# New order numbers and task times for a planned one-core kernel: gated recurrence and gated two-layer network

## The chip, the cores and the metric

The kernel runs as one launch on one core of one Trainium2 chip. The metric is the device time of that launch in microseconds (us). Five engines work side by side, each through its own queue in program order: TensorE (PE; its weight loads are listed as PEld), VectorE (DVE), ScalarE (ACT), GpSimd (POOL) and SyncE (SP), which here issues nearly all DMA transfers. An engine that comes to an instruction whose input is not ready stands there, with everything behind it.

## The reference

```python
B, H, S, D = 4, 8, 768, 48          # tokens 3072, d_model 384, d_ff 2048
for t in range(S):
    state = alpha[:, :, t, :, None] * state + k_t (outer) v_t
    y[:, :, t] = q_t @ state
x = y.transpose(0, 2, 1, 3).reshape(3072, 384)
h = x @ w_in
out = (h * tanh(softplus(h))) @ w_out
```

## The kernel before, in words

The recurrence is cut into 24 chunks (`attention(n)`, 0 to 23). Each chunk has loads of its q, k and alpha (`qka`, 772.5 KB) and v, decay products on DVE (two scans at L570 and L583, products at L579 and L593, a decay of the state at L601), and three pieces on PE: `turn` (transposes of k, L761), `scores` (L616 with the state, then L639) and `product` (L616, then L680). `scores` and `product` are 48 and 80 small matmuls in a full chunk. DVE masks the scores (L650) and adds to the state (L800); ACT and DVE split the result into a high and a low part (`xs`, L694 and L699), and SP moves rows of it (L720).

The two-layer network is cut into 105 units (`unit`, 0 to 104). A unit takes two or four chunks and one of 16 blocks of d_ff: nine matmuls on PE (`up`, L826), five passes on ACT (L835, L838, L841, L844, L853), two on DVE (`gate` L847, `lower` L856), and three matmuls per chunk on PE (`down`, L885). Tiles `t29` and `g29` are those of unit 29. Before a block can be used its weights (`ws`, 768 KB) are decoded on DVE (`w_lead`, L441, L447, L453, and `left_here`, L468), with a pass on ACT. Later each block is loaded once more (`wc`) and checked on DVE (`gathered`, L508).

While PE would have nothing to do in the first 130 us, the plan gives it fills: matmuls of a constant whose result nobody reads (L940). They stand in the program like any other instruction, so PE runs each of them when it comes to it.

The order of all engines is made while the program is built. `Plan.order` is a list scheduler: every task has a key, a cost (`COST`, occupancy and delay until its result can be used), needs and buffers, and the task that can begin first by these costs is taken next. `SHIFT` is a table of numbers added to the keys of chunks, units, weight blocks and checks, `EARLY_BANKS` says which PSUM banks a chunk takes, and `SAME` is what PE is held to save where one group of small matmuls follows another. The program's end tests a flag on every engine and leaves out a slow general path that these inputs don't need (`tc.If`, L1142).

Of the kernel before, what the change touches and what calls it, by code (L numbers as in the profile page):

```python
# [29 lines left out]
P = 128  # L30
# [4 lines left out]
NFF = FF // P  # L35
# [35 lines left out]
    0: "o1 o1 att o3 att".split(),  # L71
    1: "att o3 o1 att h".split(),
    2: "att h att att o3".split(),
    3: "o0 h att o0 o3".split(),
    4: "o2 att o3".split(),
    9: "o3 att o2".split(),
    10: "o1 o3 att".split(),
    11: "o3 o1 att".split(),
    13: "o1 o2 att".split(),
    14: "att o0 o1".split(),  # L80
    15: "o3 att att".split(),
    16: "att att o1".split(),
    17: "o2 o3 att".split(),
    18: "o3 att o0".split(),
    20: "att o3 o2".split(),
    21: "att att h".split(),
    22: "att o2 att".split(),
# [7 lines left out]
    },  # L95
    "unit": {
# [17 lines left out]
    },  # L114
    "weight": {
        0: -1.8297, 1: -88.668, 2: -1.298, 3: -0.44909, 4: -0.76088, 5: -0.16277, 7: -7.1065,
        8: -3.6601, 9: -2.0214, 11: 0.91205, 12: -0.61512, 13: 2.8687, 15: 3.8897,
    },
    "weight check": {
        1: 2.9506, 2: -1.2413, 3: -2.7653, 4: -7.2029, 5: -0.37293, 6: -5.1126, 7: -4.9684,  # L120
        8: -0.99544, 9: -8.3869, 10: -8.6038, 11: 6.855, 12: 3.149, 13: -24.555, 14: 0.49888,
        15: 1.0013,
    },
}
X_PE = 4
TURN_AT = 0.15
# [1083 lines left out]
```

## Time and profile before

| | |
|---|---|
| time, median of 3 runs | 480.56 us (480.13 to 480.57) |
| time of the profiled execution | 480.47 us, of which the span of its instructions is 478.8 us |
| PE busy | 466.8 us (97%) |
| ACT busy | 365.6 us (76%) |
| DVE busy | 340.9 us (71%) |
| granted TensorE clock | mean 0.997 of full speed |
| moved by DMA | 56.82 MB, mean 119 GB/s |

The busy time of PE holds the fills too, and its matmuls' ends are modelled, so a busy PE isn't PE at its peak. Shares over the whole span hide that the first 130 us and the rest have different limits; they are read in stretches.

### The profile page before, as it was taken

How to read it: one execution, taken by the hardware profiler on the slowest of the kernel's cores; microseconds unless marked ns; L12 is line 12 of the kernel's file. 1: busy time of each engine (PE TensorE's matmuls, PEld its weight loads, DVE VectorE, ACT ScalarE, POOL GpSimd, SP SyncE). 2: the span in 40 equal slices, each digit the busy share in tenths (PEclk: the TensorE clock that was granted, in tenths of full speed). 3: DMA queues.
4: the chain of work that ended last, by engine and by line, in shares of the span. 5: the costliest groups of instructions: out<-in, count | busy, mean ns of one | idle time of the engine just before them, and what ended most of it. 6: DMA issues, size and time to landing. Idle time of an engine off the chain costs nothing.

```text
span 478.8 us, 12662 instructions
## 1 busy us (share of the span) xinstructions
PE 466.8 (97%) x5233; PEld 418.6 (87%) x5233; DVE 340.9 (71%) x586; ACT 365.6 (76%) x816; POOL 2.4 (1%) x12
## 2 busy tenths in 40 slices
PE   7999999999999999999999989999999999999996
PEld 4668888998989889999999978999989989999995
DVE  8999999999995799789434368797376343355432
ACT  2567879889998968877887846878758878778784
POOL 2000000000000000000000000000000000000000
PEclk9999999999999999999999999999999999999998
DMA  8777536353220363154000266824252000080001
GB/s 292 247 235 253 178 127 231 135 168 115 66 67 9 129 197 111 67 184 159 0 1 0 77 223 213 318 68 132 63 183 81 1 7 4 22 291 18 0 2 70
DMA packets 20078, 56.82 MB, mean 119 GB/s; under 512 B 4016, under 2 KB 12464, under 8 KB 20016
## 3 DMA queue, kind: packets, MB, share of 16 engines
q1 hardware_dynamic: 19872, 55.77, 33.9%
q8 instruction: 42, 0.69, 0.6%
q10 hardware_dynamic: 144, 0.20, 0.1%
q14 instruction: 20, 0.16, 0.1%
HBM read 48.87 MB, written 4.72 MB: 112 GB/s over the span
## 4 chain that ended last, share of the span: by engine, by line
PE 74%; DVE 16%; ACT 6%; issue 2%; DVEq 0%
PE bank L826 31%; PE bank L885 31%; PE bank L616 4%; PE bank L940 2%; DVE t L847 2%; PE bank L639 2%; DVE rest L570 2%; PE bank L761 2%; PE bank L680 2%; DVE g L856 1%; DVE qka L583 1%; DVE w_lead L453 1%; DVE w_lead L447 1%; DVE wio L468 1%; DVE state L800 1%
## 5 line engine op out<-in xcount | busy, mean ns | idle before, releaser
L885 PE MATMUL bank<-wio,g 128*128 128x384 f32 x1152 | 207.4, 329 | 0.0
L826 PE MATMUL bank<-xs,wio 128*128 128x512 f32 (+1 forms) x945 | 205.3, 364 | 1.1 <-DVE t L847 0.8
L885 PEld LDWEIGHTS bank<-wio,g 128*128 128x128 f32 x1152 | 189.8, 189 | 5.0 <-issue 0.2
L826 PEld LDWEIGHTS bank<-xs,wio 128*128 128x128 f32 x945 | 164.0, 189 | 22.1 <-DVE t L847 3.1
L856 DVE SCALAR_TENSOR_TENSOR g<-t,g 128x512 fp32r<-128x512 f32 (+1 forms) x105 | 66.3, 642 | 55.7 <-ACT g L853 55.5
L847 DVE SCALAR_TENSOR_TENSOR t<-t,bank 128x512 f32<-128x512 f32 (+1 forms) x105 | 67.0, 638 | 48.0 <-ACT t L844 47.7
L835 ACT ACTIVATE t<-bank 128x512 f32<-128x512 f32 (+1 forms) x105 | 58.8, 560 | 48.6 <-PE bank L826 45.5
L853 ACT ACTIVATE g<-t 128x512 fp32r<-128x512 f32 (+1 forms) x105 | 60.5, 586 | 20.7 <-DVE t L847 10.6
L841 ACT ACTIVATE t<-t,fifth 128x512 f32<-128x512 f32 (+1 forms) x105 | 71.7, 684 | 2.2
L838 ACT ACTIVATE t<-t 128x512 f32<-128x512 f32 (+1 forms) x105 | 62.0, 592 | 2.1
L844 ACT ACTIVATE t<-t 128x512 f32<-128x512 f32 (+1 forms) x105 | 61.7, 588 | 1.5
L570 DVE TENSOR_TENSOR_SCAN rest<-qka,behind 112x520 f32<-112x520 f32 x24 | 29.7, 1238 | 1.3 <-DMA qka<-in_qka_dram 1.1
L583 DVE TENSOR_TENSOR_SCAN qka<-qka,ahead 112x520 f32<-112x520 f32 x24 | 29.6, 1232 | 0.0
L694 ACT ACTIVATE xs<-bank 112x256 fp32r<-112x256 f32 x48 | 15.8, 379 | 14.8 <-PE bank L680 6.9
L650 DVE COPY_PREDICATED probs<-causal,bank 128x256 f32<-128x256 uint32 x48 | 18.8, 439 | 6.8 <-PE bank L639 5.7
L835 ACT ACTIVATION_READ_ACCUMULATOR t<-bank 128x1 f32 x105 | 20.5, 195 | 0.0
L616 PE MATMUL bank<-qka,state 48*48 48x64 f32 (+1 forms) x704 | 20.0, 221 | 0.3 <-DVE qka L593 0.2
L800 DVE TENSOR_TENSOR state<-bank,state 112x192 f32<-112x192 f32 x40 | 12.9, 353 | 10.3 <-PE bank L680 6.4
L616 PEld LDWEIGHTS bank<-probs,v 64*48 64x48 f32 (+1 forms) x768 | 13.6, 127 | 7.4 <-issue 3.4
L940 PE MATMUL bank<-behind 112*128 112x384 bf16 x76 | 17.5, 367 | 2.4 <-DVE behind L362 2.4
L616 PEld LDWEIGHTS bank<-qka,state 48*48 48x48 f32 (+1 forms) x704 | 15.3, 127 | 4.8 <-issue 3.1
L508 DVE SCALAR_TENSOR_TENSOR unlike<-wc,unlike 128x768 int32<-128x768 int32 x15 | 17.0, 1134 | 3.0 <-DMA wc<-in_wp_dram 3.0
(70 smaller groups left out, 316.6 us busy)
## 6 DMA issues: line engine op xcount, KB each, us to landing
qka<-in_qka_dram SPq DMA_DIRECT2D x22, 772.5 KB, 6.0
ws<-in_wp_dram SPq DMA_DIRECT2D x16, 768.0 KB, 4.4
wc<-in_wp_dram SPq DMA_DIRECT2D x16, 768.0 KB, 5.0
v<-in_vp_dram SPq DMA_DIRECT2D x24, 192.0 KB, 3.2
out_dram<-osb SPq DMA_DIRECT2D x15, 192.0 KB, 2.3
xs<-xs SPq DMA_DIRECT2D x144, 16.0 KB, 3.6
out_dram<-part SPq DMA_DIRECT2D x8, 192.0 KB, 2.5
qka<-in_qka_dram SPq DMA_DIRECT2D x2, 260.5 KB, 3.8
```

What stands on the lines that cost most here:

```text
L570: nc.vector.tensor_tensor_scan(t[:, :0:-1], alpha()[:, :0:-1], behind[:, ::-1], 0.0, ALU.mult, ALU.max)
L583: nc.vector.tensor_tensor_scan(a, a, ahead, 0.0, ALU.mult, ALU.max)
L616: return nc.tensor.matmul(summed(x)[HALF * side : HALF * side + wide, j], weights(wide), moving, start=start, stop=stop, skip_group_check= ...
L826: nc.tensor.matmul(p[:, :N], wio[:, z, f, 0, s * P : s * P + P], by_token(x[:, s, :, a]), start=m == 0, stop=m == len(passes) - 1,)
L835: nc.scalar.activation(wide(t), wide(h), AF.Exp, accum_out=uchk[:, at : at + 1])
L838: nc.scalar.activation(wide(t), wide(t), AF.Square, bias=1.0)
L841: nc.scalar.activation(wide(t), wide(t), AF.Ln, bias=fifth, scale=0.2)
L844: nc.scalar.activation(wide(t), wide(t), AF.Exp, scale=-1.0)
L847: nc.vector.scalar_tensor_tensor(wide(t), wide(t), 2.5, wide(h), ALU.subtract, ALU.mult)
L853: nc.scalar.activation(g.tile[:, 0, :N], wide(t), AF.Copy, scale=-0.4)
L856: late[mybir.EngineType.DVE] = nc.vector.scalar_tensor_tensor(g.tile[:, 1, :N], wide(t), -0.4, g.tile[:, 0, :N].bitcast(F32), ALU.mult, AL ...
L885: made = nc.tensor.matmul(o.tile[:, :DM], g.tile[:, a, j * C : (j + 1) * C], spread(wio[:, z, f, 1]), start=begins and m == 0, stop=end an ...
```

## The change

It replaces the whole of `SHIFT` and `EARLY_BANKS`, and some task times from which the order is made. No tile, no shape and no arithmetic of the path that runs is different; the instructions are the same ones in another order, except that PE has 82 fills where it had 76. In the general path, which doesn't run, all DMAs are issued by POOL in place of SP. All lines of the file behind the tables move up by two (L826 becomes L824, and so on).

```diff
 SHIFT = {
     "chunk": {
-        0: -15.485, 1: -12.079, 2: -11.416, 3: -11.777, 4: -0.33581, 5: 1.6274, 6: -0.39491,
+        0: -25.301, 1: -20.34, 2: -13.806, 3: -11.23, 4: 4.0517, 5: 4.0522, 6: 1.3752,
...
-SAME = 0.155
+SAME = 0.33
...
-    "w seen": (1.4, 1.6),
+    "w seen": (1.6, 1.8),
...
-    "scores0": (0.65, 0.77), "scores": (0.91, 1.0), "y0": (1.12, 1.2), "y": (1.36, 1.43),
+    "scores0": (0.65, 0.77), "scores": (0.91, 1.0), "y0": (1.12, 1.2), "y": (1.39, 1.46),
...
-    COST["lead", _n] = (0.095 + 0.2 * _n, 0.17 + 0.2 * _n)
-    COST["bits", _n] = (0.114 + 0.401 * _n, 0.2 + 0.4 * _n)
+    COST["lead", _n] = (0.095 + 0.24 * _n, 0.17 + 0.24 * _n)
+    COST["bits", _n] = (0.114 + 0.435 * _n, 0.2 + 0.435 * _n)
...
-        t = add("SP", *COST["load w"], key - 4, load, uses=[again], behind=[ups[int(key)]])
+        t = add("SP", *COST["load w"], key - 4, load, uses=[again], behind=[ups[int(CHECK_FROM + f * CHECK_STEP)]])
...
             for dst, src in zip((qt, kt, vt, at), flat):
-                nc.sync.dma_start(dst, src[:, ds(t0, T), :])
+                nc.gpsimd.dma_start(dst, src[:, ds(t0, T), :])
```

**Place 1, chunk 18.** SP's queue before, from the load of chunk 18 (`qka18`) to the moves behind chunk 17 and 18 (`osb` are stores of finished chunks, `wc` loads for the weight check):

```order
L544 DMA qka18_3282<-in_qka_dram 128x1545
L497 DMA wc0_3566<-in_wp_dram 128x1536
L930 DMA out_0_dram<-osb8_3707 64x2x384
L930 DMA out_0_dram<-osb9_3717 64x2x384
L930 DMA out_0_dram<-osb10_3735 64x2x384
L930 DMA out_0_dram<-osb11_3764 64x2x384
L497 DMA wc4_3856<-in_wp_dram 128x1536
L553 DMA v18_3861<-in_vp_dram 128x384
L544 DMA qka19_3867<-in_qka_dram 128x1545
L497 DMA wc2_3871<-in_wp_dram 128x1536
L720 DMA xs0_105<-xs0_105 16x256 x12
```

SP's queue now, from the same load on:

```order
L542 DMA qka18_3377<-in_qka_dram 128x1545
L718 DMA xs1_106<-xs1_106 16x256 x6
L551 DMA v18_3508<-in_vp_dram 128x384
L542 DMA qka19_3513<-in_qka_dram 128x1545
L718 DMA xs0_105<-xs0_105 16x256 x6
L928 DMA out_0_dram<-osb8_3819 64x2x384
L928 DMA out_0_dram<-osb9_3825 64x2x384
L928 DMA out_0_dram<-osb10_3849 64x2x384
L928 DMA out_0_dram<-osb11_3851 64x2x384
L551 DMA v19_3926<-in_vp_dram 128x384
L542 DMA qka20_3930<-in_qka_dram 128x1545
L718 DMA xs0_105<-xs0_105 16x256 x6
```

The checks' loads `wc0`, `wc4` and `wc2` have left this stretch (the first check is now loaded behind chunk 22's `qka`), and chunk 19 is loaded ahead of the four stores.

PE at the same place before, from the end of chunk 18's `scores` to the head of its `product` (`g` of units 57 and 58):

```order
L639 MATMUL bank<-qka_3282 64x64 x16
L885 MATMUL bank<-wio,g_3633 128x384 x3
L761 MATMUL bank<-ident,qka_3282 128x112 x4
L885 MATMUL bank<-wio,g_3731 128x384 x6
L616 MATMUL bank<-probs_92,v_3861 48x64 x2
```

PE there now:

```order
L637 MATMUL bank<-qka_3377 64x64 x16
L759 MATMUL bank<-ident,qka_3377 128x112 x4
L883 MATMUL bank<-wio,g_3833 128x384 x3
L824 MATMUL bank<-xs_106,wio 128x512 x9
L614 MATMUL bank<-probs_92,v_3508 48x64 x2
```

Between the two pieces of chunk 18 now stand the nine wide matmuls of an `up`. Between the `product`s of chunks 16 and 17 there was one `up` and one `down` before, and there are nine `up`s and 36 `down`s now.

**Place 2, the DVE queue ahead of unit 29.** In both orders the `lower` of unit 25 is DVE's row 210, with the same instructions ahead of it. Before, from the end of `lower` 28 on:

```order
L856 SCALAR_TENSOR_TENSOR g28_1995<-t28_1937,g28_1995 128x512
L847 SCALAR_TENSOR_TENSOR t27_1977<-t27_1977,bank_1949 128x512
L468 TENSOR_TENSOR wio_104<-w_lead14_0_1966,wio_104 128x768
L856 SCALAR_TENSOR_TENSOR g27_2019<-t27_1977,g27_2019 128x512
L441 TENSOR_SCALAR w_lead13_0_2035<-ws13_1904 128x768
L583 SCALAR_TENSOR_TENSOR qka11_1715<-qka11_1715,ahead_87 112x520
L447 SCALAR_TENSOR_TENSOR w_lead13_0_2035<-ws13_1904,w_lead13_0_2035 128x768
L847 SCALAR_TENSOR_TENSOR t29_2031<-t29_2031,bank_2003 128x512
```

Now, from `lower` 27 on:

```order
L854 SCALAR_TENSOR_TENSOR g27_1991<-t27_1949,g27_1991 128x512
L451 SCALAR_TENSOR_TENSOR w_lead13_0_1977<-ws13_1866,w_lead13_0_1977 128x768
L568 SCALAR_TENSOR_TENSOR rest11_2011<-qka11_1752,behind_89 112x520
L845 SCALAR_TENSOR_TENSOR t29_1985<-t29_1985,bank_1965 128x512
L466 TENSOR_TENSOR wio_104<-w_lead13_0_1977,wio_104 128x768
L854 SCALAR_TENSOR_TENSOR g29_2033<-t29_1985,g29_2033 128x512
L439 TENSOR_SCALAR w_lead14_0_2054<-ws14_1941 128x768
```

Twelve of DVE's instructions that stood ahead of unit 29's `lower` now stand behind it: the decoding of weight block 14, the second scan and the products of chunk 11, both passes of unit 28, the `gate` of unit 30 and the first step of weight block 15.

## Rows read from the trace of the kernel before

**Rows 1.** The page, busy time of the whole span by engine.

```profile
span 478.8 us, 12662 instructions
PE 466.8 (97%) x5233; PEld 418.6 (87%) x5233; DVE 340.9 (71%) x586; ACT 365.6 (76%) x816; POOL 2.4 (1%) x12
```

**Rows 2.** Stretches: length; busy PE, PEld, DVE, ACT, POOL; clock, DMA share, GB/s.

```profile
50.00:75.00 25.00, 24.99 (x426) 22.24 (x425) 24.79 (x47) 20.28 (x52) 0.00 (x0) 1.00 0.45 155
100.00:130.00 30.00, 29.63 (x193) 27.03 (x185) 29.97 (x45) 27.58 (x59) 0.00 (x0) 1.00 0.40 137
240.00:300.00 60.00, 57.72 (x776) 52.36 (x775) 32.17 (x60) 42.82 (x93) 0.00 (x0) 1.00 0.30 108
360.00:420.00 60.00, 60.00 (x410) 55.69 (x409) 25.39 (x42) 48.71 (x102) 0.00 (x0) 1.00 0.09 27
```

**Rows 3.** Waits by engine: total us, times, longest us.

```profile
PEld bank L616 <- issue: 6.5, 17, 1.6
PE bank L616 <- issue: 1.5, 1, 1.5
PE bank L761 <- DVE qka L579: 1.0, 2, 0.6
DVE unlike L508 <- DMA wc<-in_wp_dram: 3.0, 2, 1.9
```

**Rows 4.** Timeline of 279 to 291 us: start, us, instruction, idle before it.

```profile
281.74 0.69 PE L616 MATMUL bank<-probs,v 64*48 64x64 f32 x29
...
283.92 0.26 PE L616 MATMUL bank<-probs,v 64*48 64x64 f32 x2 [1.48 <-issue]
...
284.89 0.36 DVE L800 TENSOR_TENSOR state<-bank,state 112x192 f32<-112x192 f32 x1 [2.21 <-PE bank L680]
...
288.29 0.65 DVE L579 TENSOR_TENSOR qka<-qka,rest 112x512 f32<-112x512 f32 x1
...
289.00 0.60 PE L761 MATMUL bank<-ident,qka 112*128 112x112 f32 x4 [0.56 <-DVE qka L579]
```

**Rows 5.** Stretches of 2 us around that wait, columns as above.

```profile
278.00:280.00 2.00, 2.00 (x109) 1.85 (x97) 0.95 (x3) 1.87 (x5) 0.00 (x0) 1.00 1.07 421
280.00:282.00 2.00, 1.97 (x28) 1.56 (x30) 2.00 (x5) 0.98 (x2) 0.00 (x0) 1.00 0.96 385
282.00:284.00 2.00, 0.52 (x32) 0.38 (x27) 0.69 (x2) 0.00 (x0) 0.00 (x0) 1.00 0.22 55
```

**Rows 6.** The page, a DMA queue that carries instructions: packets, MB, share.

```profile
q8 instruction: 42, 0.69, 0.6%
```

**Rows 7.** Timeline of SP, 268 to 282 us.

```profile
268.82 4.29 SPq L930 DMA_DIRECT2D out_dram<-osb  x4
273.16 0.59 SPq L497 DMA_DIRECT2D wc<-in_wp_dram  x1
274.98 0.33 SPq L553 DMA_DIRECT2D v<-in_vp_dram  x1
275.41 0.83 SPq L544 DMA_DIRECT2D qka<-in_qka_dram  x1
276.33 0.39 SPq L497 DMA_DIRECT2D wc<-in_wp_dram  x1
```

**Rows 8.** Timeline of PE: eleven fills, and a wait before unit 30's up.

```profile
9.80 1.96 PE L940 MATMUL bank<-behind 112*128 112x384 bf16 x11
...
132.24 2.21 PE L826 MATMUL bank<-xs,wio 128*128 128x512 f32 x9 [0.22 <-DVE t L847]
```

**Rows 9.** Sequencer instructions behind the flag's test and at the end.

```profile
L1142 SPq EVENT_SEMAPHORE  x8: 17/17/17, 476.4 to 477.4; - x8
...
L1205 SPq EVENT_SEMAPHORE  x10: 17/28/28, 477.5 to 478.7; - x10
```

**Rows 10.** The page, loads for the weight check: KB each, median us to landing.

```profile
wc<-in_wp_dram SPq DMA_DIRECT2D x16, 768.0 KB, 5.0
```

More of the change, by code (lines that the diff above doesn't have):

```diff
@@ L70 @@
 EARLY_BANKS = {
[L71 to L87, printed above, removed]
+    0: "att att o0 att o1".split(),
+    1: "o1 h o1 o0 o3".split(),
+    2: "att o3 o0 att h".split(),
+    3: "att o1 att o3 o0".split(),
+    4: "o3 att att".split(),
+    5: "o3 att att".split(),
+    9: "o1 att att".split(),
+    10: "att o3 o2".split(),
+    11: "o3 att att".split(),
+    12: "o2 att o3".split(),
+    13: "att o2 o0".split(),
+    14: "h att att".split(),
+    17: "o0 att att".split(),
+    18: "o1 o3 o2".split(),
+    19: "o1 att att".split(),
+    21: "att o3 o2".split(),
 }
@@ L90 @@
     "chunk": {
[4 rows of a table removed]
[4 rows of a table added]
     },
     "unit": {
[17 rows of a table removed]
[15 rows of a table added]
     },
     "weight": {
-        0: -1.8297, 1: -88.668, 2: -1.298, 3: -0.44909, 4: -0.76088, 5: -0.16277, 7: -7.1065,
-        8: -3.6601, 9: -2.0214, 11: 0.91205, 12: -0.61512, 13: 2.8687, 15: 3.8897,
+        0: 0.44719, 1: -53.48, 2: -19.485, 3: -0.79106, 4: 2.6882, 5: -2.1876, 6: -2.2027,
+        7: 4.5643, 8: 4.1694, 9: 0.97864, 10: -1.3843, 11: -0.13355, 12: -2.0257, 13: -0.16652,
+        14: 6.07, 15: 10.996,
     },
     "weight check": {
-        1: 2.9506, 2: -1.2413, 3: -2.7653, 4: -7.2029, 5: -0.37293, 6: -5.1126, 7: -4.9684,
-        8: -0.99544, 9: -8.3869, 10: -8.6038, 11: 6.855, 12: 3.149, 13: -24.555, 14: 0.49888,
-        15: 1.0013,
+        0: 1.0724, 1: 3.0549, 2: -3.8915, 3: -2.8265, 4: -14.162, 6: -10.801, 7: -0.64888,
+        8: -6.2621, 9: -0.54092, 10: -9.5662, 11: -2.1054, 12: 7.5884, 13: -5.1975, 14: 0.18778,
+        15: 2.3944,
     },
@@ L1036, in general_path @@
                 dst = x_d[b * S : (b + 1) * S, :].rearrange("t (h e) -> h t e", h=H)
-                nc.sync.dma_start(dst[:, ds(t0, T), :], yt[b * H : (b + 1) * H])
+                nc.gpsimd.dma_start(dst[:, ds(t0, T), :], yt[b * H : (b + 1) * H])
     with tc.tile_pool(name="conv", bufs=1) as sb:
@@ L1047, in general_path @@
             for m in range(2):
-                nc.sync.dma_start(
+                nc.gpsimd.dma_start(
                     t[:, m].rearrange("p c w -> p (c w)"), words[m][:, ds(c0 * 2, 2 * W)]
@@ L1072, in general_path @@
             for m in range(2):
-                nc.sync.dma_start(w_d[m][:, ds(c0, W)], f[:, m])
+                nc.gpsimd.dma_start(w_d[m][:, ds(c0, W)], f[:, m])
     with tc.tile_pool(name="moe", bufs=1) as sb, tc.tile_pool(name="pm", bufs=1, space=PSUM) as ps:
@@ L1082, in general_path @@
         as_rows = lambda t, n: t.rearrange("p c -> (p c)").rearrange("(s r c) -> r s c", s=n, r=P)
-        nc.sync.dma_start(wi, as_rows(w_d[0], NK))
-        nc.sync.dma_start(wo, as_rows(w_d[1], NFF))
+        nc.gpsimd.dma_start(wi, as_rows(w_d[0], NK))
+        nc.gpsimd.dma_start(wo, as_rows(w_d[1], NFF))
         with tc.For_i(0, B * S, P) as r0:
             x = sb.tile([P, DM], F32, name="x_g")
-            nc.sync.dma_start(x, x_d[ds(r0, P), :])
+            nc.gpsimd.dma_start(x, x_d[ds(r0, P), :])
             xT = sb.tile([P, NK, P], F32, name="xT_g")
@@ L1116, in general_path @@
             nc.scalar.copy(o, po)
-            nc.sync.dma_start(out[ds(r0, P), :], o)
+            nc.gpsimd.dma_start(out[ds(r0, P), :], o)
 @with_exitstack
```

38 rows, old and new, of the table SHIFT are left out of this document.

## The prediction

> **What bounds the kernel now.** I read the busy times of the whole span first, then the table of stretches, then the list of waits, and last the timeline around the longest wait. Over the span PE is busy for 466.8 of 478.8 us [rows 1], so all that any order can win lies in 12 us of idle PE and in the fills. The stretches show two stages. From 50 to 130 us DVE and PE are both full: DVE has 24.79 of 25.00 and 29.97 of 30.00 us [rows 2]. PE is full there partly because it runs fills, so the early stage is DVE's. Later DVE has room (25.39 of 60 us from 360 to 420) and PE is full to the last hundredth, with one exception: from 240 to 300 us it has 57.72 of 60.00 [rows 2]. The late stage is PE's, and a us of idle PE there is a us of the time, as nothing behind it has slack to give it back.
>
> That exception is nearly one wait. PE runs 29 small matmuls of chunk 18's `product` from 281.74 and starts the next at 283.92, after 1.48 us of idleness whose releaser is "issue": it waited for no semaphore that the profile shows [rows 3, 4]. The short stretches show the surroundings: DMA is at 1.07 and 0.96 of its engines until 282, then falls to 0.22, and in that last stretch PE is busy for 0.52 us, DVE for 0.69 and ACT for nothing [rows 5]. So PE stood in the middle of a group whose inputs were all there, until the transfers had drained. The page has a queue that carries instructions: 42 packets, 0.69 MB, 16.4 KB each [rows 6]. PE's 5233 matmuls [rows 1] with one weight load each are 10466 instructions, and 10466 / 42 is 249 a packet, if nearly all are PE's. One full chunk's `scores` and `product` are 128 matmuls, so 256 instructions, about one packet. I read the wait as a packet of instructions that stood in line behind data: PE uses a packet up in 2 to 3 us where small matmuls follow each other, and in some 20 us between wide ones.
>
> The line was long. SP issued four stores of 192 KB, `wc4` (768), `v18` (192), `qka19` (772.5) and `wc2` (768) from 268.82 to 276.72 us [rows 7]: 3268.5 KB, which takes 8.1 us at the 400 GB/s between the two rates of 385 and 421 [rows 5].
>
> **The change, part by part.** The instructions are the same, so their own cost cancels, and only fills, waits and the program's end are left. The sum is made from the profiled execution's 480.47 us, which is 0.09 below the median.
>
> *The wait in chunk 18.* In the new order no `wc` load stands in this stretch, and chunk 19's load is ahead of the stores (place 1). Up to `qka20` SP issues the stores, `v19` and `qka20`: 1732.5 KB, or 4.3 us at 400 GB/s in place of 8.1. PE has nine wide matmuls more between chunk 18's `scores` and `product`, and nine `up`s and 36 `down`s between the `product`s of chunks 16 and 17. So PE asks for packets later and less often while less is in line. I take the whole 1.48 us off; the bounds are 0 (the wait turns up elsewhere) and 1.62, the longest wait of the weight loads [rows 3], rounded there to 1.6.
>
> The Trainium skill speaks against this step: "Runtime: NRT & Kernel Launch", section "Instruction fetch mechanics", says that an engine streams its instructions through a DMA queue of its own in 16 KiB blocks of 256, and that crossing a block is "mostly hidden". The block's size agrees with the 16.4 KB above; that it is hidden does not fit the 1.48 us. By that rule the wait is something else, which is the first rival.
>
> *What the wait delayed.* DVE stood for 2.21 us until 284.89 for PE's `product`, with the first scan and the product of chunk 19 behind it in its queue; that product ended at 288.94, and PE then waited 0.56 us for it with chunk 19's `turn` [rows 4]. In the new order chunk 19's scans are ahead of `lower` 51 on DVE, before chunk 17 is masked. I take 0.56 off, bounds 0 and 1.0, the total of such waits [rows 3].
>
> *Six more fills.* Eleven fills take 1.96 us [rows 8], 0.18 each, so six are at most 1.1 us. They cost nothing where PE would have waited anyway. Ahead of DVE's `lower` 25 both orders have the same work on DVE, which is full, so PE can't get past the same point sooner, and some of the fills must lie in its waits. If that cover is gone, 1.1 us is added. I take 0.3.
>
> *Unit 29.* DVE's `lower` 29 has 12 instructions fewer ahead of it, and the `down`s of unit 29 can stand earlier. The trace shows only 0.22 us of wait in front of an `up` there [rows 8]. I take 0.2 off; the upper bound is the PE idleness of 100 to 130 us, 0.37 [rows 2], and the lower is 0.
>
> *The program's end.* Where the general path is skipped, SP steps through eight semaphore instructions from 476.4 to 477.4 us, and the end of the program follows on SP [rows 9]. They stand in for the DMAs that SP would have issued on the other branch. With these on POOL, the built program has none of the eight on SP, five instructions on POOL, and four more waits of SP at the very end. The eight take between nothing and the 1.0 us from first to last; four of SP's end instructions take about (478.7 - 477.5) x 4 / 9 = 0.5 us [rows 9]. So the net is between -0.5 and +0.5. Nearer to the first, as the eight run one after another, I take -0.3.
>
> *The task times* have no time of their own: they act through the order alone.
>
> The sum is 480.47 - 1.48 - 0.56 + 0.3 - 0.2 - 0.3 = 478.23, with the 0.09 back 478.3, and as new waits and removed ones of a few tenths are left out on both sides I give 478.2 us.
>
> **The rivals.** *The wait stays or moves.* Either the wait isn't an instruction packet's, or the new order has another place where about a packet's worth of small matmuls meets loads: `qka20`, `qka21` and `qka22` (772.5 KB each) are now issued among chunks 17 to 19. Against it speaks that each is 1.9 us of transfer at 400 GB/s and not 8.1. The time is then 478.2 + 1.48 + 0.56 = 480.2 us. The rule of the Trainium skill named above speaks for this case.
>
> *More goes.* The early stage gets faster too. PE has 0.01 and 0.37 us of idleness in the two early rows [rows 2], and the six fills say that the plan expects idleness and not less of it; but the small groups' other 16 "issue" waits are 6.5 - 1.6 = 4.9 us [rows 3], 0.3 each, and an order that sets small groups together loses some. Against it: counted in the two orders, 8 of the 48 `scores` and `product` followed another such group before, and 9 do now, which is one wait of 0.3. If 2 us more go in all, the time is 476.2.
>
> *Slower: the checks stand in front of the units.* The first seven `wc` loads are now issued together behind `qka22`, and DVE has their seven `gathered` between the `gate`s of units 66 to 73. A load takes 5.0 us to land [rows 10] and there are two buffers, so DVE may stand in front of a check, with `gate` and `lower` of the next units behind it, and PE waits for these. In the trace the longest such wait was 1.9 us [rows 3]. It decides from the point at which DVE's delay exceeds the lead of a `lower` over its first `down`. With two such waits of 1.9 on the path the time is 478.2 + 3.8 = 482.0 us. Against it: eight units are at least 25 us of PE (60.00 us for 410 matmuls from 360 to 420 [rows 2], 0.146 each, with small ones among them, and 21 per unit of four chunks), against 4 x 5.0 = 20 us for seven loads in two buffers.
>
> **How the numbers follow.** A measurement of this kernel can tell a change of about 0.2%, 0.96 us, from none: faster is below 479.6, slower above 481.5. The forecast (476.8 to 479.6) has a chance of 0.50. More goes (below 476.8) 0.17. The wait stays or moves (479.6 to 481.5) 0.18. Slower, by the checks or by fills and a moved wait together, 0.15. So faster is 0.67, same 0.18 and slower 0.15. The range is 475.6 to 481.2: it holds the bounds of the sum (480.47 - 1.6 - 1.0 - 0.4 - 0.5 = 477.0 and 480.47 + 1.1 + 0.5 = 482.1, hardly all at once), reaches below for the second rival, and leaves out most of the slow case. The forecast's own range is 476.8 to 479.6.
>
> **What would show it.** The wait's step is right if the list of waits has no "issue" wait above 0.5 us on PE, and PE is full from 240 to 300 us to within 0.5. If such a wait stands beside a DMA share near 1 in another chunk, the first rival holds. The step on fills is right if DVE's `lower` 25, which ends at the same row of its queue, comes within 0.3 us of its time before and PE is as full until 130 us. The end is right if the eight semaphore instructions are gone from SP and the time from the last matmul to the span's end is shorter by 0.3. The slower rival would show as DVE waiting for `wc` for more than 3 us in total. The prediction is wrong if PE waits in the early stage for DVE by more than 1 us over before, or if the idle PE of the late stage is as long as before.

## The result

The changed kernel takes 476.19 us (median of 6 runs, 475.45 to 477.52) against 480.27 us before (480.12 to 480.57): a ratio of 0.990, 95% interval 0.9882 to 0.9919. That is 4.1 us less by the medians and 3.9 to 5.7 by the interval. The forecast of 478.2 us was 0.5% below the 480.56 that it started from; 1.0% was measured, and 476.19 lies below the forecast's own range of 476.8 to 479.6, in the part that the prediction calls "more goes" (a chance of 0.17). The profiled execution is the slowest of the six: 477.52 us, a span of 476.0, so 3.0 us below the profiled one before.

The page of the changed kernel, the line that answers to [rows 1]:

```profile
PE 465.8 (98%) x5239; PEld 419.5 (88%) x5239; DVE 340.7 (72%) x586; ACT 363.4 (76%) x816; POOL 2.4 (1%) x12
```

Its stretches, which answer to [rows 2]:

```profile
50.00:75.00 25.00, 23.94 (x493) 20.75 (x492) 24.80 (x46) 17.28 (x44) 0.00 (x0) 1.00 0.42 145
100.00:130.00 30.00, 29.93 (x234) 27.23 (x233) 30.00 (x46) 27.57 (x61) 0.00 (x0) 1.00 0.39 134
240.00:300.00 60.00, 60.00 (x676) 55.29 (x676) 39.23 (x70) 48.36 (x104) 0.00 (x0) 1.00 0.31 107
360.00:420.00 60.00, 60.00 (x410) 55.78 (x409) 26.86 (x43) 46.27 (x97) 0.00 (x0) 1.00 0.21 72
```

The stretch from 240 to 300 us is now full, which is what the prediction asked for. From 50 to 75 us PE has 1.05 us less than before.

Its waits, which answer to [rows 3] (total us, times, longest):

```profile
PEld bank L614 <- issue: 4.5, 16, 0.5
DVE unlike L506 <- DMA wc<-in_wp_dram: 4.4, 3, 1.9
...
PE bank L824 <- DMA xs<-xs: 1.0, 1, 1.0
PE bank L614 <- DVE probs L648: 0.9, 1, 0.9
...
PE bank L883 <- DVE g L854: 0.8, 1, 0.8
```

No "issue" wait of PE is left, and no wait of `turn` (L759 now). Three others are there: an `up` waits for chunk 3's moves at 41 us, chunk 6's `product` for its mask at 65, and unit 38's `down` for its `lower` at 184. DVE waits for the weight checks for 4.4 us in total, more than the 3 us that the slower rival named, and nothing comes of it, since PE is full behind 300 us (30.00 of 30.00 us in each stretch of 30 us up to 420).

**Two marks divide the gain.** The two orders have exactly the same matmuls ahead of unit 26's `up`, but for the six fills, and again ahead of unit 104's, the last. So the starts of these two groups say how far PE has got. The timeline of PE, before:

```profile
117.00 2.21 PE L826 MATMUL bank<-xs,wio 128*128 128x512 f32 x9
...
463.90 2.11 PE L826 MATMUL bank<-xs,wio 128*128 128x512 f32 x9
```

The changed kernel, first profile:

```profile
117.28 2.10 PE L824 MATMUL bank<-xs,wio 128*128 128x512 f32 x9
...
461.40 2.10 PE L824 MATMUL bank<-xs,wio 128*128 128x512 f32 x9
```

The changed kernel, a second profile (run e8 below, 475.6 us):

```profile
115.53 2.10 PE L824 MATMUL bank<-xs,wio 128*128 128x512 f32 x9
...
459.48 2.11 PE L824 MATMUL bank<-xs,wio 128*128 128x512 f32 x9
```

From mark to mark it is 463.90 - 117.00 = 346.90 us before, 344.12 and 343.95 now: the late stage gives 2.8 to 3.0. Between the marks the busy and the idle time of PE can be told apart (the ends of matmuls are modelled, so the border between the two is not sharp). Before, and the first profile of the changed kernel:

```profile
117.00:463.90 346.90, 344.16 (x3541) 316.43 (x3541) 223.32 (x375) 273.01 (x577) 0.00 (x0) 1.00 0.27 93
```

```profile
117.28:461.40 344.12, 343.35 (x3542) 316.17 (x3541) 224.22 (x376) 271.93 (x578) 0.00 (x0) 1.00 0.29 96
```

The idle time falls from 2.74 to 0.77 us, and the busy time of the same matmuls by 0.8, which no wait of PE shows.

From the second mark to the span's end it is 14.9 us before and 14.6 now, 0.2 less by the unrounded times. The first mark has to be counted from PE's first matmul and not from the span's first instruction: that matmul stands at 2.38 us before and at 2.61 now, while the time outside the span is shorter by as much (see e3). Counted so, the first mark is at 114.62 us before, at 114.67 in the first profile and at 112.92 in the second: no lead and 1.7 us. The three parts add up: 2.8 + 0.2 - 0.05 = 2.95 us, where the first profiled execution is 2.95 below that of before, and 2.95 + 0.2 + 1.7 = 4.85, where the second is 4.87 below. So the late stage and the end give 3.0 to 3.2 us in either run, and what differs between runs of the changed kernel lies ahead of 117 us. A third such mark is chunk 2's `product`: it starts 20.87 us behind PE's first matmul before, and 19.91 and 19.23 in the two profiles, so the lead is there by then, and the first profile loses it again at 41 us.

### The profile page after: what moved, and what is told of

Read it like the earlier page. It is cut to its first block, busy times and chain, and to the rows that moved or that the text cites. A ratio compares the mean times of both kernels' runs of the same rounds, so it can differ in the third digit from the quotient of the medians.

```text
span 476.0 us, 12661 instructions
## 1 busy us (share of the span) xinstructions
PE 465.8 (98%) x5239; PEld 419.5 (88%) x5239; DVE 340.7 (72%) x586; ACT 363.4 (76%) x816; POOL 2.4 (1%) x12
## 4 chain that ended last, share of the span: by engine, by line
PE 89%; DVE 6%; DMA 2%; ACT 1%; issue 1%; SPq 0%; DVEq 0%
PE bank L824 37%; PE bank L883 37%; PE bank L614 5%; PE bank L938 2%; PE bank L637 2%; PE bank L678 2%; PE bank L759 2%; DMA xs<-xs 1%; DMA qka<-in_qka_dram 1%; DVE qka L581 1%; DVE rest L568 1%; DVE w_lead L451 1%; DVE g L854 1%; DVE t L845 0%; DVE w_lead L445 0%
## 5 line engine op out<-in xcount | busy, mean ns | idle before, releaser
L824 PE MATMUL bank<-xs,wio 128*128 128x512 f32 (+1 forms) x945 | 204.9, 365 | 1.1 <-DMA xs<-xs 1.0
L883 PE MATMUL bank<-wio,g 128*128 128x384 f32 x1152 | 203.8, 328 | 0.8 <-DVE g L854 0.8
L824 PEld LDWEIGHTS bank<-xs,wio 128*128 128x128 f32 x945 | 164.3, 189 | 20.8 <-DVE t L845 1.4
L938 PE MATMUL bank<-behind 112*128 112x384 bf16 x82 | 19.2, 367 | 2.6 <-DVE behind L360 2.6
```

Of the source, the lines that this page charges most:

```text
L824: nc.tensor.matmul(p[:, :N], wio[:, z, f, 0, s * P : s * P + P], by_token(x[:, s, :, a]), start=m == 0, stop=m == len(passes) - 1,)
L883: made = nc.tensor.matmul(o.tile[:, :DM], g.tile[:, a, j * C : (j + 1) * C], spread(wio[:, z, f, 1]), start=begins and m == 0, stop=end an ...
```

## The experiments

Each run was compared with runs of the kernel before on its own chip, where that kernel had medians of 481.2 to 482.3 us. Ratios, not microseconds, are to be set beside 0.990. In most of them the planner's order is replaced by a list of its tasks in a fixed order; where the list is the kernel's own, each engine's queue is that kernel's, instruction by instruction.

### The issue wait, and chunk 19's turn

**e4: two of the loads late.** The order of before, with the loads of `wc4` and `wc2` and their two DVE instructions moved from 273 to 277 us to some 440. On SP:

```diff
 four stores
-L497 DMA wc4 128x1536
 L553 DMA v18 128x384
 L544 DMA qka19 128x1545
-L497 DMA wc2 128x1536
 L720 DMA xs x12
...
+L497 DMA wc4 128x1536   (behind the check of f14)
+L497 DMA wc2 128x1536   (behind the check of f15)
```

> The order of before; only two of the weight checks' loads (wc4 and wc2, 768 KB each) and their gathered instructions are moved, from SP's stretch of 273 to 277 us to some 440 us. PE's order is that of before, instruction by instruction. Theory (a packet of PE's instructions stands behind queued data): 1.5 of the 3.3 MB are gone from the line, so the 1.48 us wait in chunk 18's product goes to under 0.5, and with the follow-on wait the time falls by 1.5 to 2.5 us, to 477.8 to 478.8. Rival (the wait has nothing to do with transfers): the wait stays at 1.2 to 1.6 us and the time at 480.0 to 480.5.

Measured: ratio 0.9958 (0.9939 to 0.9976), 479.76 us against 481.57. Its timeline of PE, which answers to [rows 4]:

```profile
282.41 0.69 PE L616 MATMUL bank<-probs,v 64*48 64x64 f32 x32
...
283.72 1.24 PE L885 MATMUL bank<-wio,g 128*128 128x384 f32 x6
...
287.95 0.60 PE L761 MATMUL bank<-ident,qka 112*128 112x112 f32 x4 [0.56 <-DVE qka L579]
288.32 0.73 PE L885 MATMUL bank<-wio,g 128*128 128x384 f32 x3
```

The 32 small matmuls run through without a break. From the `product`'s first matmul to the `down` behind it PE takes 1.31 us, where it took 281.74 to 284.77, 3.03 us, before: 1.7 less. The transfers of the stretch show the instruction packet itself. Before, the q8 packet began at 281.56 us and took 0.96, so that it ended just as PE came to a stop, at 282.4:

```profile
q8 instruction: 1, 0.02, 4.0%
```

In e4 it falls into 280 to 281.5 us, more than 2 us ahead of the group, though the group comes 0.7 us later than before:

```profile
q8 instruction: 1, 0.02, 4.6%
```

So the wait was for a packet of PE's own instructions, and with less data in line the packet comes sooner. The other traces agree: in each of the eleven "issue" waits of PE of 0.4 us or more (here and in e1, e3, e5, e7, e10, e13, e15 and e17) PE goes on 1.2 to 1.8 us after such a packet has ended. And `turn` still waits its 0.56 us, as before: that wait was no follow-on of the first one.

**e7: e4, and chunk 19's first scan earlier on DVE.**

```diff
+scan_rest c19, inverse c19, mult_k c19
 gather c18a, gather c18b
 lower c18a, lower c18b
-scan_rest c19, inverse c19, mult_k c19
```

> e4 (order of before, the loads wc4 and wc2 late) with one more move: chunk 19's first scan, its reciprocal and its product on DVE stand ahead of chunk 18's gather instead of behind chunk 18's lower. In e4 the wait of chunk 19's turn stayed at 0.56 us although the issue wait was gone, so it was no follow-on of it. Theory: that wait is DVE's order, so it goes now, and with it 0.5 to 0.7 us against e4; two more tenths may go with the next wait at 294 us. Rival: the load of chunk 19 lands too late for it, and the wait stays or moves to DVE's scan: same time as e4.

Measured: ratio 1.0011 (0.999 to 1.0031), as slow as the kernel before. Its timeline of PE:

```profile
286.69 0.55 PE L761 MATMUL bank<-ident,qka 112*128 112x112 f32 x4
287.01 0.73 PE L885 MATMUL bank<-wio,g 128*128 128x384 f32 x3
...
346.75 0.33 PE L616 MATMUL bank<-qka,state 48*48 48x64 f32 x7
349.27 0.36 PE L616 MATMUL bank<-qka,state 48*48 48x64 f32 x9 [2.20 <-issue]
```

`turn` waits no longer. From the `up` ahead of it (284.80 in e4, 284.26 here) to the `down` behind it PE takes 2.75 us and not 3.52: the wait was DVE's order, and is worth 0.77. But an issue wait of 2.20 us has come up in chunk 20's `product` (the later expectations call it chunk 22's, which is a slip), and takes more than the move gave.

**e15: e7, and `wc10` late too.** The load of `wc10`, which e7 issued at 342.58 us between the stores of that stretch, stands behind `wc8`'s.

> e7 with a third load, wc10 of 768 KB, moved from the stretch ahead of chunk 22's product to behind wc8's. Theory: the issue wait of 2.2 us at 347 us goes as the one of chunk 18 went in e4, and the wait of chunk 19's turn (0.56 us) stays away, so the time is 0.5 to 1.0 us below e4's, a ratio of 0.993 to 0.995. Rival: the issue wait is a matter of where PE's instructions are in their blocks and not of that load; it stays or moves, and the ratio is 0.998 to 1.002 as in e7.

Measured: ratio 1.0049 (1.0028 to 1.0071). Its timeline of PE:

```profile
347.87 0.37 PE L616 MATMUL bank<-qka,state 48*48 48x64 f32 x9 [0.67 <-issue]
...
367.53 1.78 PE L826 MATMUL bank<-xs,wio 128*128 128x512 f32 x7 [3.24 <-DVE t L847]
```
With 768 KB less in the line the issue wait at the same instruction falls from 2.20 to 0.67 us, which is the theory's direction and not all of its size. The whole theory on the time failed: the load that was moved now stands, with `wc8`'s, at 357.51 us ahead of nine moves on SP (359.41 to 366.63), and an `up` that reads `xs` stands for 3.24 us. The view names DVE as its releaser; that the late moves are behind it is my reading and wasn't tried by itself.

**e10: two loads put back into the changed kernel.**

```diff
 L542 DMA qka20 128x1545
+L495 DMA wc0 128x1536
+L495 DMA wc4 128x1536
 L718 DMA xs x6
```

> The changed kernel with two checks' loads (wc0 and wc4, 768 KB each) moved from behind chunk 22's load to right behind chunk 20's load, so that the line on SP's queue is as long as it was before: four stores, v19, qka20 and the two loads, 3268.5 KB. Theory A (the line alone decides): an issue wait of 0.5 to 1.7 us comes back among chunks 17 to 20, and the time rises by 1 to 2.5 us over the changed kernel. Theory B (PE asks for fewer packets there, as wide matmuls stand between its small groups): no issue wait above 0.3 us; chunk 18's moves stand behind the two loads, which costs 0 to 1 us if an up waits for them.

Measured: ratio 0.9938 (0.9917 to 0.9958), some 2 us above the changed kernel. Its timeline of PE:

```profile
282.77 0.57 PE L614 MATMUL bank<-probs,v 64*48 64x64 f32 x22
283.78 0.38 PE L614 MATMUL bank<-probs,v 64*64 64x64 f32 x9 [0.44 <-issue]
```

The issue wait is back, at a third of its old length with the same 3268.5 KB in line. The profile is of the fastest of the eight runs (476.54 us, where their median is 478.28), and from mark to mark it takes 345.03 us, 1.0 more than the changed kernel; what the slower runs lost isn't seen. Both theories had a part: the line brings the wait, and that PE's order decides how much of it shows is the likely reason for the shorter one.

### How the gain divides

Seven kernels join the two orders at a seam: up to it the one order, behind it the other, without what is done already. Ahead of the seam each queue is that of the first kernel.

```diff
-    tasks = plan.order()
+    first, then = ORDER_A[:seam], ORDER_B
+    tasks = first + [t for t in then if t not in first]
```

**e1, e2: the seam at 110 us.**

> The new order up to unit 24's up (some 110 us, with its six more fills), the order of before behind it, the general path's transfers on SP as before. Theory: the late stage and the end carry only the 2.3 us that the prediction gave them, and the rest of the measured 4.1 us comes from the early stage, some 1.3 to 1.8 us; so 478.5 to 479.0 us, with the issue wait of chunk 18 still there. Rival: the early order brings nothing, since its six fills eat what it saves, and the late stage brings it all: 480.0 to 480.6 us.

> The order of before up to unit 24's up (some 110 us), the new order behind it, the general path's transfers on SP as before. Theory: the issue wait of chunk 18 goes, and the follow-on wait of chunk 19's turn, with a few tenths more: 2.0 to 2.6 us, so 477.7 to 478.3 us, and PE full from 240 to 300 us. Rival (the late stage brings it all): 476.0 to 476.6 us.

Measured: e1 1.0067 (1.0043 to 1.0091), e2 1.0002 (0.9973 to 1.0031). Neither can be read: the one order had prepared weight 12 by then and the other weight 9, and PE stands right behind the seam. e1's longest wait of PE from 105 to 117 us:

```profile
PE bank L885 <- ACT g L853: 2.0, 1, 2.0
```

**e5, e6: the seam at 178 and at 156 us.**

> As e1, with the seam at 178 us instead of 110, where PE is full and DVE is not, so that the seam itself should cost nothing (in e1 it cost 2.8 us of idle PE at 110 to 113 us). Theory: the new order up to 178 us brings 1.0 to 1.8 us (a time of 0.996 to 0.998 of before), as part of the gain lies there. Rival: it brings nothing or costs up to 1 us, as the six more fills are paid for (1.000 to 1.002), and the late stage carries all of the 4.1 us.

> As e2, with the seam at 156 us. Theory: the new order from 156 us on brings the waits of the late stage, 1.48 + 0.72 + 0.38 + 0.37 less what new waits cost: 2.0 to 3.0 us (0.9935 to 0.996 of before). Rival (all of the gain is late): 3.8 to 4.8 us, 0.990 to 0.992.

Measured: e5 1.0104 (1.0073 to 1.0135), e6 0.9931 (0.9909 to 0.9953). e5's seam stalled too, with DVE 2.48 us in front of a chunk's load. e6 ends between the theory's 0.9935 to 0.996 and the rival's 0.990 to 0.992, nearer to the first, and its interval reaches into both.

**e9: the first 19 us old, the rest new.**

> The changed kernel with the order of before up to chunk 2's turn (some 19 us), the new order behind it. In e8's profile PE had done 0.9 us more of its own matmuls by 30 us than the kernel before. Theory: this lead lasts to the end, so without it the time is 0.6 to 1.0 us above the changed kernel's, a ratio of 0.990 to 0.992. Rival: DVE is what holds the early stage, the lead is lost to it later, and the ratio is that of the changed kernel, 0.988 to 0.990.

Measured: 1.0012 (0.9991 to 1.0033). Again the seam: weight 2 is asked for there and at once waited for. The waits of e9's first 30 us:

```profile
DVE w_lead L439 <- DMA ws<-in_wp_dram: 5.0, 1, 5.0
...
PE bank L614 <- DVE probs L648: 3.5, 1, 3.5
```

It answers another question, though. Unit 26's `up` starts at 121.78 in e9, 6.25 us after e8's, and unit 104's at 465.36, 5.88 us after e8's. What is lost at 20 us isn't given back by 465. (Not all of it is the wait: behind it the granted clock falls, see the last section.)

**e13, e14: the seam at 124 and at 121 us,** where the orders differ by two or three instructions that no weight and no load hangs on.

> As e1 and e5, with the seam at 124 us behind unit 26's gate, where the two orders differ by three instructions that no load or weight hangs on. Theory: the new early order brings 1.0 to 2.0 us, a ratio of 0.996 to 0.998, with no new wait above 0.7 us at the seam. Rival: nothing or a loss, 1.000 to 1.003, as the fills are paid for and what e8's profile shows as a lead at 130 us is lost again to DVE.

> As e2 and e6, with the seam at 121 us behind chunk 10's second scan. Theory: the late part alone brings 2.0 to 3.0 us, a ratio of 0.9935 to 0.996. Rival: all of it, 0.988 to 0.991.

Measured: e13 1.0048 (1.0021 to 1.0074), e14 0.9922 (0.9895 to 0.9948). The marks in e14's timeline, and the first one in e13's:

```profile
116.93 2.21 PE L826 MATMUL bank<-xs,wio 128*128 128x512 f32 x9
...
460.37 2.11 PE L826 MATMUL bank<-xs,wio 128*128 128x512 f32 x9
```

```profile
115.50 2.11 PE L826 MATMUL bank<-xs,wio 128*128 128x512 f32 x9
```

e14 is the cleanest of the seven: the first mark is where it was before, and from mark to mark it takes 343.44 us, 3.5 less. The new late order alone brings 0.8%, between the theory's 2 to 3 us and the rival, and the interval reaches both; e18 below, which has the same late order, takes 344.79 us from mark to mark, with 1.0 us of wait for a `lower` at 184 us that e14 has not. In e13 PE reaches the first mark 1.5 us sooner, and loses it behind the seam: it waits 2.2 us for DVE's `gate`s (three waits from 117 to 140 us), later 0.7 and 0.8 us for two more, and the granted clock falls behind its issue wait (last section). That is the rival's time. It suggests that the lead of the early stage counts only with the new order behind it; more can't be said, as the seam brings waits of its own.

**e8: the changed kernel once more.**

> The changed kernel itself once more, for a second profile and for its time beside the others on one chip. Its first profiled run was its slowest, 2.0 us over its fastest. Theory: the early waits for transfers (1.0 us at 41 us for chunk 3's moves, 0.9 at 65, 0.9 at 183) differ from run to run and one or two of them are missing or shorter here; ratio 0.988 to 0.992. Rival: they stay, and the spread lies in the start or the end.

Measured: 0.9883 (0.9854 to 0.9912), 476.0 us against 481.95. The wait for chunk 3's moves is missing in its profile; its `up` starts at 40.69 us there and at 42.46 in the first one. The other two waits stay (0.9 and 0.7 us). Seven profiles have the order of before ahead of unit 26's `up` (the first one, e3, e4, e6, e7, e14, e15): it starts 114.2 to 115.0 us behind PE's first matmul, 114.6 in the middle. Seven have the new one (the two of the changed kernel, e5, e10, e13, e16, and e11 but for fills): 112.8 to 114.7, 113.2 in the middle, so 1.4 sooner. The two latest of these, the first profile (114.67) and e11 (114.13), are the ones that wait longest for chunk 3's moves, 1.0 and 0.7 us.

### Single terms

**e3: the end alone.** The order of before; in the general path `nc.sync.dma_start` becomes `nc.gpsimd.dma_start`, as in the change.

> The order of before throughout; only the general path's transfers are moved from SP to POOL. Theory: the end is shorter by the eight semaphore instructions less four waits, 0.3 us, so 480.0 us. Rival: what SP no longer steps through turns up in its last waits, 480.3 us. If the move also changed something at the program's beginning, the time would be off by more than 0.5 us.

Measured: 0.9998 (0.9978 to 1.0018). The interval can't tell 0.3 us, but the trace can. Sequencer instructions of the changed kernel at the end, which answer to [rows 9] (count: ns, first to last us):

```profile
L1140 POOLq EVENT_SEMAPHORE  x5: 17/43/43, 473.9 to 474.2; - x5
...
L1203 SPq EVENT_SEMAPHORE  x14: 17/28/28, 474.4 to 476.0; - x14
```

The eight are gone from SP, and from unit 104's `up` to the span's end it is 14.64 us now and 14.62 in e3, 14.87 before: the end gives 0.2. At the program's beginning, e3 and then the kernel before:

```profile
L1195 POOLq MOVE  x5: 29/29/35, 0.1 to 0.4; - x5
...
2.61 1.76 PE L940 MATMUL bank<-behind 112*128 112x384 bf16 x5 [2.61 <-DVE behind L362]
```

```profile
L1195 SPq MOVE  x4: 29/34/42, 0.0 to 0.2; - x4
...
2.38 2.08 PE L940 MATMUL bank<-behind 112*128 112x384 bf16 x6 [2.38 <-DVE behind L362]
```

Four `MOVE`s that opened the span on SP stand on POOL now, ahead of its first work; the other engines begin with it, and PE's first matmul comes 0.23 us later in the span. But less of the time lies outside the span: the profiled execution takes 1.70 us more than its span before, 1.48 in e3 and 1.47 in the changed kernel. That and the time to PE's first matmul are 4.09 us together in all three, so the beginning costs nothing that the time shows, and the 0.2 of the end stay.

**e11: eight fills fewer.** Three ahead of chunk 6's `scores`, four ahead of chunk 7's, one at 80 us.

> The changed kernel without its last eight fills (three before chunk 6's scores, four before chunk 7's, one at 80 us). Theory: these stand in waits of PE for DVE, so that they cost nothing: the ratio stays that of the changed kernel within 0.001, and waits of 0.5 to 0.7 us appear in their places. Rival: each costs its 0.16 us, and the time falls by 1.0 to 1.3 us. If the granted clock falls in the places without fills, the time rises.

Measured: 0.9891 (0.9867 to 0.9916), as the changed kernel. Two waits of `scores` stand in their places, by PE's waits from 60 to 75 us:

```profile
PE bank L614 <- DVE state L599: 0.5, 1, 0.5
PE bank L614 <- DVE qka L591: 0.4, 1, 0.4
```

The fills cost nothing that shows.

**e17, e18: six early fills out.** The order of before has six fills between chunk 2's `turn` and its `scores`, the new one has none there. e17 is the kernel before without these six, e18 is e14 without them.

```diff
 L761 MATMUL bank<-ident,qka x4
-L940 MATMUL bank<-behind x6
 L616 MATMUL bank<-qka,state x16
```

> The kernel before without the six fills between chunk 2's turn and its scores (20.09 to 21.06 us), and nothing else. Theory: they stood in front of scores that could have begun, so PE is 0.8 to 1.0 us sooner at chunk 2's product and at unit 26's up, and the time is 0.5 to 1.0 us lower, a ratio of 0.998 to 0.999 (the late issue wait stays). Rival 1: the scores weren't ready; the fills' place becomes a wait, the marks stay within 0.2 us. Rival 2: the lead is there at chunk 2's product and lost to DVE by unit 26's up.

> e14 (order of before up to 121 us, the new one behind it) without the same six fills. Theory: these six and the late order are most of the change: unit 26's up at 115.9 to 116.2 us in place of e14's 116.93, and a ratio of 0.989 to 0.991, between e14's 0.992 and the changed kernel's 0.988 to 0.990. Rival: the ratio stays at e14's 0.992.

Measured: e17 1.0085 (1.0065 to 1.0106), slower by 4 us for six matmuls fewer; e18 0.9926 (0.9907 to 0.9944), as e14. The timeline of e17 at the place, and its waits of PE:

```profile
20.12 0.46 PE L616 MATMUL bank<-qka,state 48*48 48x64 f32 x16
20.99 0.69 PE L639 MATMUL bank<-qka 48*64 48x64 f32 x32 [0.41 <-ACT ks L765]
...
22.86 0.34 PE L616 MATMUL bank<-probs,v 64*48 64x64 f32 x8
```

```profile
PE bank L616 <- issue: 3.7, 2, 2.2
```

From `turn` to `product` it is 3.21 us (19.65 to 22.86), where it was 3.55 before (19.70 to 23.25) and is 2.73 in both profiles of the changed kernel. So the fills cost 0.3, and the rest of their place becomes a wait for ACT: rival 1, nearly. The new order doesn't have that wait. Before, and then the changed kernel:

```profile
20.42 0.58 ACT L765 COPY ks<-bank 128x448 f32<-128x448 f32 x1
...
21.41 0.66 PE L639 MATMUL bank<-qka 48*64 48x64 f32 x32
```

```profile
20.50 0.58 ACT L763 COPY ks<-bank 128x448 f32<-128x448 f32 x1
20.53 0.66 PE L637 MATMUL bank<-qka 48*64 48x64 f32 x32
```

ACT copies `turn`'s result (`ks`) 0.7 us behind the start of `turn` in both, but the second group of `scores` begins behind that copy before and beside it now. The reason is in `EARLY_BANKS`: chunk 2 had the PSUM banks `att h att att o3`, three uses of the two `att` buffers, and in the built program that group writes the bank that `turn` wrote and waits for ACT's copy; with `att o3 o0 att h` it writes another bank and waits for nothing of ACT. The 3.55 us are the same in all eight profiles with the old order there (3.54 in two of them), the 2.73 in all nine with the new (2.74 in one): 0.8 us, of which the fills are 0.3. On DVE the mask of chunk 2 also stands ahead of a decoding step (L451) that was ahead of it before. No run changed the banks alone.

Unit 26's `up` starts at 117.20 us in e17 and 116.91 in e18, no sooner than with them. e17 takes 4.0 us more than before from mark to mark, and 2.2 of them are a second issue wait, in chunk 20's `product` like e7's, beside the old 1.5. Twelve PE instructions fewer (six matmuls with their weight loads) move every later boundary between packets, which would explain a new wait; that is argued and not shown.

**e12: two moves that should help.** On SP chunk 5's two loads behind chunk 3's six moves; on DVE unit 38's `lower` ahead of unit 39's `gate`.

> The changed kernel with two pieces of its order changed: chunk 3's six moves stand ahead of chunk 5's two loads on SP, and unit 38's lower ahead of unit 39's gate on DVE. Theory: PE's wait for the moves at 41 us (1.0 us in the first profile of the changed kernel, none in the second) is gone in every run, and the wait for lower 38 at 182 us is 0.1 to 0.3 instead of 0.7 to 0.9: 0.5 to 1.2 us less than the changed kernel, a ratio of 0.986 to 0.989. Rival: chunk 5's scan waits for its later load, DVE is full there, and the time rises by 0.5 to 1.5 us.

Measured: 0.9918 (0.9894 to 0.9941), no better than the changed kernel. The rival held: in its timeline DVE stands for the later load, and PE for DVE.

```profile
43.56 1.24 DVE L568 TENSOR_TENSOR_SCAN rest<-qka,behind 112x520 f32<-112x520 f32 x1 [2.11 <-DMA qka<-in_qka_dram]
...
45.18 1.89 PE L883 MATMUL bank<-wio,g 128*128 128x384 f32 x10 [1.25 <-DVE g L854]
```

**e16: the second of them alone.**

> The changed kernel with unit 38's lower ahead of unit 39's gate on DVE, and nothing else. Theory: the wait for lower 38 at 182 us falls from 0.7 to 0.9 us to under 0.3, and the time by 0.4 to 0.7 us: a ratio 0.001 below the changed kernel's. Rival: unit 39's lower becomes the late one and the wait only moves by a unit: no change.

Measured: 0.9906 (0.9878 to 0.9935). The wait for unit 38's half on DVE is gone, and 0.29 us for ACT's half stands in its place, but unit 26 to unit 104 takes 344.59 us, no less than in the two profiles of the changed kernel. No gain shows. None of the versions tried beats the changed kernel.

## Why the prediction was wrong in size

The direction, the wide range and the main mechanism were right; the forecast's own range was missed. The size was half of what was measured, and the step that failed is the one on the early stage; the late stage gave 2.8 to 3.0 us, where the sum had 2.24.

- **What bounds the kernel: half right.** The late stage is PE's, as read: what goes there goes from the time (e14). The early stage was put down to DVE alone, from two rows that begin at 50 us. Ahead of 50 us DVE isn't full (17.04 of 18 us from 12 to 30), and the changed order wins there: its lead at chunk 2's `product` is 1.0 and 1.6 us in the two profiles, counted from PE's first matmul.
- **The step that failed: "PE can't get past the same point sooner".** `lower` 25 on DVE, which the prediction set as the mark of this, starts at 122.52 us before, at 123.50 and 121.75 in the two profiles of the changed kernel. It was to be within 0.3. The sum gave the early stage +0.3 for the fills; it is -1.4 by the middle value of the first mark, and nothing only in the slowest run. Here "more goes" was right, and its own reason, the small groups' issue waits, has a small share at most: these fell from 6.5 to 4.5 us in total, and 1.6 of that is the one long wait. What the step left out is that DVE's work ahead of the mark isn't all that PE waits for: between chunk 2's `turn` and `product` PE takes 2.73 us in place of 3.55 in every profile with the new order, since `scores` no longer waits for ACT to empty a bank and six fills are out of the way. `EARLY_BANKS`, which does the first of these, has no term in the prediction. That is 0.8 of the 1.4. Where the rest lies stays open, and how the 0.8 reaches the first mark isn't isolated: without the six fills alone the lead of 0.3 was gone by unit 26 (e17, e18), and the seams that were to show it stalled by themselves or lost the lead behind them.
- **The issue wait: right, -1.48 forecast, -1.7 measured (e4).** It is an instruction packet behind data, and one comes back where loads come back (e10), in chunk 20 when PE reaches that place earlier (e7), and there again when six fills are out (e17). The first rival was right in one thing: it can move. The Trainium skill ("Runtime: NRT & Kernel Launch", "Instruction fetch mechanics") calls the crossing of a block mostly hidden. The traces agree with "mostly": of the 42 packets of a run none to two show as such a wait, of 0.4 to 2.2 us. (The page's KB are of 1024 bytes, so the prediction's 3268.5 KB take 8.4 us at 400 GB/s and not 8.1, which changes nothing.)
- **"What the wait delayed": the price too low, the reason wrong.** The 0.56 us of `turn` is not the wait's delay, as it stays in e4; it is chunk 19's place on DVE, and e7 shows 0.77 for it.
- **Unit 29 and the "few tenths left out on both sides": too small.** e14's late gain of 3.5 us less 1.7 and 0.77 leaves 1.0, where the sum had 0.2. PE's idle time between the marks is 2.74 us before and 0.21 in e14, so 0.5 of it lay in short waits besides the two named. In the changed kernel the new wait for unit 38's `lower`, which nobody had on the list, takes 0.7 to 0.8 back.
- **"The instructions are the same, so their own cost cancels": not quite.** Between the marks the same matmuls keep PE busy for 344.16 us before, 343.35 and 343.29 in the changed kernel and 343.23 in e14. The sum had nothing for these 0.8 to 0.9 us. What makes them is not shown.
- **Fills: 0.3 forecast, none seen** for the last eight (e11) and 0.3 for six others at their place, lost again by unit 26 (e17).
- **The end: right, -0.3 forecast, -0.2 measured.** The later start of PE in the span is made up for outside it (e3).
- **The slower rival** was wrong where it mattered: DVE waits 4.4 us for the checks, and PE's stretches behind 300 us are full.

With the terms as measured the sum is 480.47 - 2.8 - 0.2 - 1.4 = 476.1 us, near the median. The term of 1.4 is a middle value over seven profiles and runs from -1.8 to nothing, about the spread of the changed kernel's own runs (2.07 us).

## What to carry to other kernels

Where PE stops in the middle of a group with all inputs there, look for a packet of its instructions in the 3 us before it goes on, and for what was issued to the DMA queues in the 8 us before that; take the loads away from there, and then look whether such a wait has come up elsewhere, as it did here with a change of DVE's order (e7) and with six fills taken out (e17). Don't call a stage another engine's from its fullest rows: check the stretch ahead of it, read what each table of the change hands out, the banks too, and set marks that have the same work ahead of them in both orders. And an order is one piece: in three of three cases (e1, e5, e13) the better order's beginning with the other's end was slower than either alone, though in two of them the seam itself stalled.

## What the hardware showed unasked

A wait costs more than itself when the granted clock falls after it. In e1 the issue wait of chunk 18 was 1.59 us and ended at 285.53. Stretches of 2 us behind it (PE, PEld, DVE, ACT, POOL; then the clock):

```profile
284.00:286.00 2.00, 0.47 (x33) 0.47 (x36) 0.38 (x1) 0.00 (x0) 0.00 (x0) 1.00 0.13 33
286.00:288.00 2.00, 2.00 (x46) 1.95 (x37) 0.67 (x3) 0.66 (x2) 0.00 (x0) 0.69 0.11 25
288.00:290.00 2.00, 2.00 (x7) 1.73 (x6) 1.97 (x5) 0.00 (x0) 0.00 (x0) 0.50 0.08 18
290.00:292.00 2.00, 2.00 (x12) 1.75 (x12) 2.00 (x4) 0.07 (x1) 0.00 (x0) 0.96 0.48 120
```

The same is in e13, where the wait was 1.83 us and ended at 285.81: 0.67, 0.50 and 0.97 in the stretches from 286 to 292. It is also in e9 behind its wait of 3.5 us (0.75 and 0.50 from 26 to 30 us) and in e5 behind its seam (0.50 from 182 to 184), so parts of what these runs lost are clock. At 0.50 the clock is at 1.2 GHz. In e1 the six `down`s behind the wait take 2.12 us and 1.24 in e4, the nine matmuls of the next `up` 2.96 and 2.10: 1.7 us more, as much as the wait. In the profiled run before, the same wait of 1.48 us left the clock at 1.00 in every stretch of 2 us from 282 to 294, and so did 2.20 us in e7 (347 to 357), 2.19 in e17 (350 to 358) and a wait of 3.24 us for DVE in e15 (364 to 372). So the length of the wait alone doesn't decide it. Over the 97 runs of the kernel before beside e1 to e16, the 23 with a mean clock of 0.995 or less have a median of 483.5 us, the 29 with 0.999 or more 481.1. That fits a wait which in some runs brings the clock down and in others doesn't; the changed kernel, without it, has 0.997 to 1.000 in all of its runs. It may be why the ratio was 0.9883 beside these runs and 0.990 in the first comparison, but of the kernel before itself there is no profile of such a run, so this is argued and not shown.
